# Memory attention and SwiGLU on one core: keys and values of the last four batches handled inside the first sweep, and one sweep for each of the last two pairs

## The chip, the cores and the metric

The kernel runs on one core of one Trainium2 chip. The metric is the device time of one execution in microseconds (us). The kernel before takes 942.52 us, the median of three runs that lie between 942.49 and 943.4. About 0.2% is what a measurement of this kernel can tell from no change.

A core has engines with queues of their own: TensorE (PE, matmuls and transposes; PEld are its weight loads), VectorE (DVE), ScalarE (ACT), GpSimd (POOL) and SyncE (SP), which here issues all transfers. Each queue is worked off in the order in which it was written. Matmuls write to PSUM, which PE, DVE and ACT reach; all else is in SBUF.

## The reference, cut to what matters

Eight batches, 8 heads, 576 rows, head size 64, 32 memory slots; then a SwiGLU layer with 512 inputs and 1536 hidden units on all 4608 rows:

```python
a = softmax(phi, axis=2)                       # over the 576 rows
k_m, v_m = a^T k, a^T v                        # 32 x 64 for each batch and head
attn = softmax(q k_m^T / 8, axis=-1)           # 576 x 32
x = attn v_m                                   # heads side by side: 4608 x 512
xn = x / sqrt(mean(x*x) + 1e-6) * rms_g
out = (silu(xn @ w_gate) * (xn @ w_val)) @ w_out
```

The three weights come as 64-bit floats. TensorE works in a 32-bit form in which a number is carried as a high and a low part, so each large product is three matmuls (high-high, high-low, low-high).

## The kernel before, in words

The batches are worked in four **pairs** (two batches each). `v_m` is never multiplied out over the rows: for each pair and each block of 128 hidden units the kernel first multiplies `v_m` with the weights (tile `vp`, lines 837 to 869), and then the attention weights of the pair (`at_hi`, `at_lo`) with that product (tiles `pg` and `pv`, lines 871 to 915).

**Part 1** (lines 428 to 821) does, for all eight batches, the keys and values: load `phi`, `k`, `v`; take the maximum of `phi` over rows (`prep`: DVE reduce `mc`, PE transpose `mt`, DVE `mx` and `mb`, PE transpose `mr`, DVE subtract, ACT exp into `e_bd`, POOL partial sums `es`); 72 matmuls into `kvp` and 24 for the sums (`kv_steps`); DVE `si`, `im`, `kb`, `vb`; PE transposes `kvt`; copies to `km` and `vt`. For batches 4 to 7, `km` stays in SBUF (`km_late`), and the rest goes to DRAM. For pairs 0 and 1 it also does queries, scores, softmax and `x_steps`, which ends in a short chain of small DVE instructions for `rinv` (lines 257 to 278), three transposes `rp`, and the split into `at_hi` and `at_lo`.

**The sweeps** (lines 824 to 1088) are 48 steps of 128 hidden units for one pair: pairs 0 and 1 in turn through all 12 blocks (steps 0 to 23, the first sweep), then pairs 2 and 3 in turn (steps 24 to 47). In each step PE does 12 matmuls for `vp`, 48 for `pg` and `pv`, and every two steps 54 for the output (`po`). `vp` has one buffer; ACT copies it to `xf` in three instructions and casts it to `xh`, POOL subtracts for `xl` (`evac`, lines 858 to 868). DVE multiplies `pv` with the activated `pg` into `hf` and adds `po` to `acc`; `pg`, `pv` and `po` have two buffers each.

Inside the first sweep run two more things. **Weight conversion** (`convert`, lines 335 to 414): 36 pieces of 512 columns are turned from 64-bit floats into the two parts; a piece is seven instructions on DVE. Converted weights are also written to DRAM and read back (`reload`) in the second sweep. **Attention of pairs 2 and 3** (`attend_steps`, `x2`).

Every step has a place on a time axis (tables in `PRM`), and the steps are issued in that order; a scheduler then puts the instructions of an engine into a fixed order of its own, by its own model of when each can run. The tables were written for that.

Of the kernel before, what the change touches and what calls it, by code (L numbers as in the profile page):

```python
# [19 lines left out]
WB = 3  # L20
PRM = dict(
    K_AT=[12.08, 15.05, 41.68, 67.52, 100.72, 122.69, 147.6, 167.28],
    KP=0.82,
    POST=[-0.15, 3.05, 3.9, 7.72, 15.27, 21.96],
    P1=4.13,
    PREP=[-1.56, 0.79, 2.32, 3.9, 18.7],
    PD=[2.1, 11.67, 7.79, 18.42, 7.54, 2.17],
    EXP=[1.89, 13.89, 3.07, 6.96, 11.93, 1.72],
    ES=1.16,
    PH=[9.86, 15.89, 41.23, 73.43, 103.91, 132.92],  # L30
    S_AT=[32.67, 47.44, 51.02, 69.42, 103.56, 112.2, 119.41, 123.39],
    KD=[-29.43, -117.84, -35.71, -6.98, -5.97, -14.4, 0.19, -2.47, -27.9, -16.32, -19.75, -7.2, -11.66, -11.87, -26.49, -25.1, -22.49, -18.77, -23.35, -24.43, -11.42, -13.48, -5.56, -9.46, -16.01, -22.32, -10.3, -18.0, -66.41, -9.39, -2.35, -17.36],
    QD=[5.05, 0.01, 25.98, 0.89, 23.44, 5.14, 27.93, 20.58],
    PD0=0.96,
# [3 lines left out]
    SO=[3.76, 13.53, 20.6, 28.62],  # L38
    X_AT=[102.5, 152.9],
    XP=1.78,  # L40
    LAG=0.79,
    CV=114.79,
    CP=3.53,
    CV2=155.67,
    CP2=0.05,
# [3 lines left out]
    ESN=[3, 3, 2, 3, 3, 3, 2, 3],  # L49
    QX=[2, 8],  # L50
# [13 lines left out]
    SU=[1.874, 3.014, 5.716, 6.6, 9.746, 12.208, 13.357, 15.533],  # L64
    AO=[0.162, 0.169, 0.192, 0.276, 0.385, 0.474, 0.562, 0.581, 0.59, 0.601, 0.728, 0.804, 1.158, 1.217],
    XB=[17.199, 22.916],
    XS=[0.1086, 0.0359],
    XM=[21.887, 24.858],
    XN=[0.012, 0.176, 0.184, 0.33, 0.33, 0.566, 0.596, 0.699, 0.766],
    LV=[22.571, 24.198],  # L70
# [21 lines left out]
def kernel(  # L92
# [44 lines left out]
    gram = {}  # L137
    gb = persist.tile([P, 2, 2, P], F32, name="gb")
# [171 lines left out]
    def first_weights():  # L310
        return (
            [lambda: (load_w(0, 0), load_w(1, 0))]
            + convert(0, 0) + [lambda: load_w(0, 1)] + convert(1, 0) + [lambda: load_w(1, 1)]
        )
# [101 lines left out]
    def reload(kind, n):  # L416

        if kind == 2:
            t = [wp[1].tile([P, 512], F32R, tag=x, name=f"{x}{n}", bufs=2) for x in ("oh", "ol")]
# [8 lines left out]
    with ExitStack() as c1:  # L428
# [6 lines left out]
        ones = sb.tile([P, 1], F32, name="ones", bufs=1)  # L435
        nc.vector.memset(ones, 1.0)
        hmask = sb.tile([P, 2], F32, name="hmask", bufs=1)
# [10 lines left out]

        rg = [sb.tile([P, HP], F32, name=f"rg{i}", bufs=1) for i in range(2)]
# [51 lines left out]
        def prep(b, hp0=0, hp1=HP):  # L501
# [55 lines left out]
            def s4():  # L557
                e = e_bd[b % 2]
                n = PRM["ESN"][b]
# [12 lines left out]
        def kv_steps(b):  # L572
# [59 lines left out]
            def post2():  # L632
                tp = st.pop(("kvt", b))
                km = km_late.get(b)
                if km is None:
                    km = sb.tile([P, HP, 64], F32, tag="km", name=f"km{b}", bufs=4)
# [482 lines left out]
```

## Time and profile before

| stage (us from the start) | PE busy | DVE busy | granted PE clock |
|---|---|---|---|
| part 1, 0 to 158 | 118.2 | 114.3 | 0.87 |
| 158 to 200 | 31.3 | 38.1 | 0.84 |
| 200 to 450 | 224.4 | 205.7 | 0.98 |
| 450 to 569 | 113.5 | 61.8 | 0.97 |
| second sweep, 569 to 940.2 | 364.6 | 140.4 | 1.00 |

The profiled execution took 941.95 us in all, and its span from first to last instruction is 940.2 us; 1.75 us lie around it. The first `pg` matmul of step 0 starts at 158.2 us, and that of step 24 at 569.2 us; these two moments bound the first sweep. A row of the profile names line, engine, operation and tile; "busy, mean ns | idle before <- who ended it" follows. PE busy is no measure of useful work, since matmuls overlap.

### The profile page before, as it was taken

The page shows a single profiled execution, that of the slowest core. Times are in us where ns is not written, and L with a number is a line of the kernel's source. Part 1 is how long each engine was busy: PE and PEld are TensorE (multiplying, and loading weights), DVE is VectorE, ACT ScalarE, POOL GpSimd, SP SyncE. Part 2 cuts the span into 40 slices and gives each one's busy share as a digit, 9 for nine tenths or more (in the row PEclk, how much of TensorE's full clock was granted, in tenths as well). Part 3 has the DMA queues.
Part 4 walks back from the last instruction along what each step waited for, and adds up shares of the span by engine and source line. Part 5 has one row for each costly group of instructions (what it writes and reads, how often), then busy time and mean ns, then how long its engine had stood idle before and what let it go on. Part 6 is the DMA issues. An engine that isn't in the chain of part 4 may idle for free.

```text
span 940.2 us, 15899 instructions
## 1 busy us (share of the span) xinstructions
PE 852.0 (91%) x6207; PEld 756.7 (80%) x6207; DVE 560.4 (60%) x998; ACT 433.2 (46%) x743; POOL 408.7 (43%) x290
## 2 busy tenths in 40 slices
PE   5799676689889899897799999999999999999998
PEld 4678565679779688786699898798989999999996
DVE  5487969895897976969843463643333333333333
ACT  2566333656547546465454354343343443443430
POOL 2365636562653554454344354253333423433421
PEclk9889877899899999999899999999999999999999
DMA  8997644452343623434223215341202212030046
GB/s 282 254 288 237 225 134 131 143 159 66 98 158 83 187 76 83 161 100 152 90 64 102 68 60 134 85 115 45 90 1 69 67 36 100 1 129 7 1 107 140
DMA packets 85667, 106.42 MB, mean 113 GB/s; under 512 B 38996, under 2 KB 56920, under 8 KB 85592
## 3 DMA queue, kind: packets, MB, share of 16 engines
q1 hardware_dynamic: 85592, 105.41, 37.7%
q8 instruction: 49, 0.80, 0.4%
q14 instruction: 26, 0.21, 0.1%
HBM read 73.93 MB, written 31.46 MB: 112 GB/s over the span
## 4 chain that ended last, share of the span: by engine, by line
PE 69%; DVE 20%; DMA 3%; issue 3%; ACT 3%; POOL 1%; SPq 0%; DVEq 0%; ACTq 0%; POOLq 0%
PE po L931 28%; PE pv L889 13%; PE pg L889 13%; PE vp L852 5%; DVE mi L369 3%; DVE mi L365 3%; DVE w L385 2%; PE kvp L583 2%; PE xp L235 2%; DVE ex L345 2%; DMA phi<-in_phi_dram 2%; DVE ex L358 1%; DVE acc L938 1%; DVE ex L357 1%; DVE ex L352 1%
## 5 line engine op out<-in xcount | busy, mean ns | idle before, releaser
L912 POOL TENSOR_TENSOR hl<-hf,hh 128x512 fp32r<-128x512 f32 (+1 forms) x96 | 143.6, 1496 | 235.1 <-ACT hh L911 180.6
L938 DVE TENSOR_TENSOR acc<-po,acc 128x512 f32<-128x512 f32 x180 | 123.8, 689 | 165.4 <-PE po L931 165.2
L931 PE MATMUL po<-oh,hh 128*128 128x512 f32 x432 | 174.4, 405 | 14.3 <-DVE acc L938 12.0
L867 POOL TENSOR_TENSOR xl<-xf,xh 128x1024 fp32r<-128x1024 f32 x48 | 118.3, 2465 | 137.4 <-ACT xh L866 73.6
L931 PE MATMUL po<-oh,hl 128*128 128x512 f32 x432 | 172.0, 398 | 0.0
L931 PE MATMUL po<-ol,hh 128*128 128x512 f32 x432 | 171.5, 397 | 0.0
L897 ACT ACTIVATE sg<-pg 128x256 f32<-128x256 f32 x192 | 78.5, 411 | 189.3 <-PE pg L889 175.5
L898 DVE TENSOR_TENSOR hf<-pv,sg 128x256 f32<-128x256 f32 x192 | 85.4, 452 | 106.9 <-PE pv L889 65.2
L931 PEld LDWEIGHTS po<-oh,hh 128*128 128x128 f32 x432 | 81.7, 190 | 30.5 <-DVE acc L938 15.3
L889 PE MATMUL pv<-ath,xh 128*128 128x320 f32 (+1 forms) x384 | 87.2, 306 | 15.6 <-DVE hf L898 15.6
L852 PE MATMUL vp<-wh,vm 128*128 128x256 f32 x384 | 89.0, 297 | 11.1 <-ACT xf L863 10.8
L931 PEld LDWEIGHTS po<-oh,hl 128*128 128x128 f32 x432 | 81.9, 190 | 19.5
L911 ACT CAST hh<-hf 128x512 fp32r<-128x512 f32 (+1 forms) x96 | 64.6, 674 | 70.7 <-DVE hf L898 40.0
L931 PEld LDWEIGHTS po<-ol,hh 128*128 128x128 f32 x432 | 82.0, 190 | 10.9
L889 PE MATMUL pg<-ath,xh 128*128 128x320 f32 (+1 forms) x384 | 87.2, 302 | 1.1 <-ACT sg L897 1.1
L889 PE MATMUL pg<-ath,xl 128*128 128x320 f32 (+1 forms) x384 | 85.7, 298 | 0.0
L889 PE MATMUL pg<-atl,xh 128*128 128x320 f32 (+1 forms) x384 | 85.7, 299 | 0.0
L889 PE MATMUL pv<-atl,xh 128*128 128x320 f32 (+1 forms) x384 | 83.8, 298 | 0.0
L889 PE MATMUL pv<-ath,xl 128*128 128x320 f32 (+1 forms) x384 | 83.7, 296 | 0.0
L889 PEld LDWEIGHTS pv<-ath,xh 128*128 128x128 f32 x384 | 63.6, 193 | 23.0 <-DVE hf L898 18.4
L852 PEld LDWEIGHTS vp<-wh,vm 128*128 128x128 f32 x384 | 68.8, 201 | 14.1 <-ACT xf L863 11.7
L889 PEld LDWEIGHTS pg<-ath,xh 128*128 128x128 f32 x384 | 64.9, 192 | 7.3 <-ACT sg L897 1.5
(133 smaller groups left out, 1522.7 us busy)
## 6 DMA issues: line engine op xcount, KB each, us to landing
kv<-in_k_dram SPq DMA_DIRECT2D x32, 288.0 KB, 6.2
kv<-in_v_dram SPq DMA_DIRECT2D x32, 288.0 KB, 6.2
out_dram<-acc SPq DMA_DIRECT2D x72, 128.0 KB, 2.4
raw<-in_moe_w_gate_dram SPq DMA_DIRECT2D x12, 512.0 KB, 4.1
raw<-in_moe_w_val_dram SPq DMA_DIRECT2D x12, 512.0 KB, 4.1
wd<-wh SPq DMA_DIRECT2D x12, 512.0 KB, 3.5
wd<-wl SPq DMA_DIRECT2D x12, 512.0 KB, 3.3
raw<-in_moe_w_out_dram SPq DMA_DIRECT2D x12, 512.0 KB, 3.6
```

Of the source, the lines that this page charges most:

```text
L235: nc.tensor.matmul(xp[64 * j:64 * j + 64, P * cc:P * cc + P], st["at"][:, t, cc, 64 * j:64 * j + 64], gb[:, j, cc], start=True, stop=True,)
L365: V.tensor_scalar(out=m, in0=d["raw"][:, :, 1], scalar1=0xFFFFF, scalar2=None, op0=ALU.bitwise_and)
L369: V.scalar_tensor_tensor(out=mf, in0=d["raw"].bitcast(U32)[:, :, 0], scalar=2.0 ** -32, in1=m, op0=ALU.mult, op1=ALU.add,)
L852: nc.tensor.matmul(vp[:, cc, e, :], lhs(l), r[:, 2 * cc + e, :], start=(n == 0), stop=(n == 2),)
L867: nc.gpsimd.tensor_tensor(out=xl, in0=xf, in1=xh.bitcast(F32), op=ALU.subtract)
L889: nc.tensor.matmul(pt[:, :N], l[:, cc, b, half * P:half * P + P], r[:, b, cc, t0:t0 + n, :].rearrange("p t x -> p (t x)"), start=(m == 0), ...
L897: nc.scalar.activation(sg[:, :N], pg[:, :N], AF.Silu)
L898: nc.vector.tensor_tensor(out=hf[:, :, b, :], in0=pv[:, :N].rearrange("p (t x) -> p t x", x=64), in1=sg[:, :N].rearrange("p (t x) -> p t x ...
L911: nc.scalar.copy(hh, hv)
L912: nc.gpsimd.tensor_tensor(out=hl, in0=hv, in1=hh.bitcast(F32), op=ALU.subtract)
L931: nc.tensor.matmul(po, l[:, tt, :], r, start=(m == 0), stop=(m == 5))
L938: nc.vector.tensor_tensor(out=accs[key], in0=po, in1=accs[key], op=ALU.add)
```

## The change

- Part 1 handles batches 0 to 3 only. Loads come in a fixed list, 1.1 units apart.
- Keys and values of batches 4 to 7 are done by the new `late_kv` in the first sweep, at steps 0.3, 2.1, 9.5 and 11.3. It shares PSUM buffers with `po`, and holds two of a batch's four (k, v) tiles at a time, in the buffers `qr` and `qT`, so the second half is fetched when the first has been used.
- Pairs 2 and 3 have a sweep each (steps 24 to 35 and 36 to 47). Converted weights are now read back for each of the 24 steps instead of for 12 blocks.
- `evac`: `xf` is gone. For each half of the partitions ACT casts `vp` to `xh`, and DVE, no longer POOL, subtracts for `xl`, straight from PSUM.
- The tables of times are new, buffers for converted weights `w` go from three to two, and some choices of part 1 that were set batch by batch are uniform.

```diff
-WB = 3
+WB = 2
-    K_AT=[12.08, 15.05, 41.68, 67.52, 100.72, 122.69, 147.6, 167.28],
+    K_AT=[12.0, 22.0, 36.0, 46.0],
-    X_AT=[102.5, 152.9],
-    XP=1.78,
+    X_AT=[47.5, 73.5],
+    XP=0.87,
+    KV=[0.3, 2.1, 9.5, 11.3],
...
-    NS = (NP // G) * NU * G * 2
+    NS = NP * NJ
+    UNITS = [(p, u) for u in range(NU) for p in range(G)] + [(p, u) for p in range(G, NP) for u in range(NU)]
...
         def evac():
             vp = vw[i][0]
-            xf = sb.tile([P, 2, 2, 256], F32, tag="xf", name=f"xf{i}")
-            nc.scalar.copy(xf[0:64], vp[0:64])
-            for b in range(2):
-                nc.scalar.copy(xf[64:128, :, b, :], vp[64:128, :, 1 - b, :])
...
-            nc.scalar.copy(xh, xf)
-            nc.gpsimd.tensor_tensor(out=xl, in0=xf, in1=xh.bitcast(F32), op=ALU.subtract)
+            for h in range(2):
+                rows = slice(64 * h, 64 * h + 64)
+                src = vp[rows, :, ::-1, :] if h else vp[rows]
+                nc.scalar.copy(xh[rows], src)
+                nc.vector.tensor_tensor(out=xl[rows], in0=src, in1=xh[rows].bitcast(F32), op=ALU.subtract)
...
+    def late_kv(b):
...
+        def fetch_kv(cc):
+            def f():
+                for par in range(2):
+                    hp = 2 * cc + (par ^ j)
+                    d[par] = t = sb.tile([P, 2, S], F32, tag=("qr", "qT")[par], name=f"kv{b}_{hp}")
+                    for i, src in enumerate((k, v)):
+                        nc.sync.dma_start(
...
+        def mm(cc):
+            def f():
+                d["kvp"] = kvp = o_tile(f"kvp{b}_{cc}")
+                for c in range(NT):
+                    for par in range(2):
+                        nc.tensor.matmul(
+                            kvp[64 * par:64 * par + 64, 0:128], late["e"][:, 2 * cc + (par ^ j), c, :],
+                            d[par][:, :, 64 * c:64 * c + 64], start=(c == 0), stop=(c == NT - 1),
+                        )
+            return f
...
+        return [
+            lambda: (fetch_phi(), fetch_kv(0)()), top, turn_mc, top2, turn_mb, less, exp, some,
+            mm(0), sums(0), norm(0), fetch_kv(1), mm(1), sums(1), norm(1), turn, post, self_products, post2,
+        ]
...
-    NALL = (NP // G) * NJ
...
+        n = where(i)[3]
+        if n >= NJ:
+            ev.append((i - PRM["WR"], lambda n=n: reload(0, n)))
+            ev.append((i - i % 2 - PRM["OR"] + 0.01 * (i % 2), lambda n=n: reload(2, n)))
...
+    for a, p in enumerate(PRM["KV"]):
+        ev += place(p, PRM["KO"], late_kv(2 * G + a))
```

How the change moves instructions is seen best at two places. The first is VectorE's queue at the end of part 1, in the middle of the chain for `rinv` of pair 1 (lines 274 to 276 in both kernels), on which `rp`, the split of pair 1 and, by PE's order, the first `vp` wait. Before:

```order
L274 TENSOR_TENSOR u_1666<-rinv_71 128x9
L275 TENSOR_TENSOR u_1666<-u_1666,m_1660 128x9
L276 SCALAR_TENSOR_TENSOR rinv_71<-u_1666,rinv_71 128x9
L274 TENSOR_TENSOR u_1666<-rinv_71 128x9
L606 TENSOR_SCALAR si_1746<-kvp_1621 128x2
L275 TENSOR_TENSOR u_1666<-u_1666,m_1660 128x9
L607 RECIPROCAL si_1746<-si_1746 128x2
L276 SCALAR_TENSOR_TENSOR rinv_71<-u_1666,rinv_71 128x9
```

After (`raw`, `ex`, `mi`, `w` are tiles of weight conversion; the number behind the name is the block):

```order
L275 TENSOR_TENSOR u_1302<-u_1302,m_1296 128x9
L384 TENSOR_TENSOR w_1_1571<-mi_1_1565,ex_1_1554 128x512
L276 SCALAR_TENSOR_TENSOR rinv_75<-u_1302,rinv_75 128x9
L344 TENSOR_SCALAR ex_2_1718<-raw_1398 128x512
L364 TENSOR_SCALAR mi_2_1728<-raw_1398 128x512
L274 TENSOR_TENSOR u_1302<-rinv_75 128x9
L351 TENSOR_SCALAR ex_2_1718<-ex_2_1718 128x512
L368 SCALAR_TENSOR_TENSOR mi_2_1728<-raw_1398,mi_2_1728 128x512
L275 TENSOR_TENSOR u_1302<-u_1302,m_1296 128x9
L356 TENSOR_SCALAR ex_2_1718<-ex_2_1718 128x512
L276 SCALAR_TENSOR_TENSOR rinv_75<-u_1302,rinv_75 128x9
```

Between the links of the chain now stand instructions of four weight pieces; ahead of the first `hf` of the sweep nine pieces are begun, where seven were begun before.

The second place is TensorE's queue in step 1, the second half of its `pg` and `pv` (L889 before, L875 after). Before:

```order
L889 MATMUL pv_01_1995<-ath_1393,xl_1900 128x256 x2
L889 MATMUL pg_10_2016<-ath_1393,xh_1899 128x320 x2
L889 MATMUL pg_10_2016<-atl_1394,xh_1899 128x320 x2
L889 MATMUL pg_10_2016<-ath_1393,xl_1900 128x320 x2
L889 MATMUL pv_10_2017<-ath_1393,xh_1899 128x320 x2
```

After (`kvp` is the product of `e_late` with the keys and values `kv` of batch 4; `ones` stands for the sums):

```order
L875 MATMUL pv_01_1578<-ath_1158,xl_1466 128x256 x2
L1019 MATMUL kvp_0_1598<-kv_1_1456,e_late 64x128
L1031 MATMUL kvp_0_1598<-ones,es_1573 64x1 x2
L1031 MATMUL kvp_0_1598<-ones,e_late 64x1
L1031 MATMUL kvp_0_1598<-ones,es_1573 64x1 x2
L1031 MATMUL kvp_0_1598<-ones,e_late 64x1
L1019 MATMUL kvp_1_1656<-kv_2_1632,e_late 64x128
L875 MATMUL pg_10_1639<-ath_1158,xh_1465 128x320 x2
```

The matmuls of batch 4 now stand between those of the sweep, and the first one of the second half (`kvp_1`, which reads the newly fetched `kv_2`) stands directly behind the last ones of the first half, ahead of the rest of step 1.

259 lines of the change are left out of this document (175 added, 84 removed).

## The prediction

> **What bounds the kernel now.** I read the slices of the page first, then busy time by stage, then what ended TensorE's idle time, then single stretches. The slices are 23.5 us each:
>
> ```profile
> PE   5799676689889899897799999999999999999998
> DVE  5487969895897976969843463643333333333333
> DMA  8997644452343623434223215341202212030046
> ```
>
> For the first two slices the transfers are full and DVE is half idle; from the third on DVE is the fuller one, and DMA falls. The stages in numbers:
>
> ```profile
> core 0: us, PE busy (x) PEld busy (x) DVE busy (x) ACT busy (x) POOL busy (x), PEclk, DMA share, GB/s
> 0.00:158.00 158.00, 118.19 (x1497) 101.44 (x1497) 114.31 (x240) 71.73 (x130) 80.20 (x87) 0.87 0.74 221
> 158.00:200.00 42.00, 31.27 (x184) 29.14 (x182) 38.12 (x46) 22.96 (x39) 24.77 (x14) 0.84 0.47 155
> 200.00:450.00 250.00, 224.42 (x1540) 198.86 (x1541) 205.73 (x330) 141.26 (x232) 118.27 (x71) 0.98 0.40 118
> 450.00:569.00 119.00, 113.52 (x748) 100.19 (x747) 61.77 (x125) 54.77 (x99) 53.32 (x41) 0.97 0.27 87
> 569.00:940.20 371.20, 364.58 (x2244) 327.08 (x2242) 140.43 (x261) 142.46 (x245) 132.10 (x79) 1.00 0.24 68
> ```
>
> The second sweep is PE end to end (6.6 us idle of 371), so nothing is to be won there, and its work doesn't change. The first sweep runs from here to here:
>
> ```profile
> 158.19 0.79 PE L889 MATMUL pg<-ath,xh 128*128 128x256 f32 x2
> 569.21 0.40 PE L889 MATMUL pg<-ath,xh 128*128 128x256 f32 x2
> ```
>
> In its 411 us PE is busy 369.2 and idle 41.8, and the idle time has these owners (groups of PE in that stretch):
>
> ```profile
> L931 PE MATMUL po<-oh,hh 128*128 128x512 f32 x186 | 76.8, 413 | 13.2 <-DVE acc L938 10.9 <-DVE ex L1006 1.4 <-DVE acc L936 0.4
> L852 PE MATMUL vp<-wh,vm 128*128 128x256 f32 x201 | 46.3, 299 | 6.1 <-ACT xf L863 6.1
> L889 PE MATMUL pv<-ath,xh 128*128 128x256 f32 (+1 forms) x192 | 45.9, 316 | 15.2 <-DVE hf L898 15.2
> L995 PE MATMUL S<-km,qT 128*64 128x64 f32 x288 | 11.7, 227 | 5.7 <-DVE acc L938 2.6 <-DVE acc L936 2.5 <-ACT qT L983 0.6
> ```
>
> So the first sweep is PE-bound, with DVE late by a tenth. Why late, one case shows:
>
> ```profile
> 239.17 2.82 POOL L867 TENSOR_TENSOR xl<-xf,xh 128x1024 fp32r<-128x1024 f32 x1
> 239.79 2.48 DVE L345 TENSOR_SCALAR ex<-raw 128x512 int32<-128x512 int32 x1
> 244.13 0.80 PE L889 MATMUL pv<-ath,xh 128*128 128x256 f32 x2 [3.27 <-DVE hf L898]
> ...
> L345 DVE TENSOR_SCALAR ex<-raw x36: 359/428/2648, 88.2 to 460.2; 128x512 int32<-128x512 int32 x36
> L938 DVE TENSOR_TENSOR acc<-po,acc x180: 628/692/693, 285.3 to 935.5; 128x512 f32<-128x512 f32 x180
> ```
>
> A conversion instruction of 0.43 us takes 2.48 beside POOL's `xl` of 2.82 us, and `hf` behind it is late; `acc`, which reads PSUM, never lasts over 0.69.
>
> **Term 1, part 1 and the start of the sweep: -12 us.** Removed from DVE are four batches, each by these rows an eighth of 38.6 us (the first two are over nine instructions), so 4.8:
>
> ```profile
> L509 DVE TENSOR_REDUCE mc<-phi 128x128 f32<-128x1152 f32 (+1 forms) x9 | 17.4, 1937 | 6.8 <-DMA phi<-in_phi_dram 6.8
> L542 DVE TENSOR_TENSOR phi<-phi,mr 128x1152 f32<-128x1152 f32 (+1 forms) x9 | 11.0, 1217 | 12.1 <-PE mr L533 12.1
> L609 DVE TENSOR_TENSOR im<-si,hmask 128x4 f32<-128x4 f32 x8 | 3.5, 441 | 0.1
> L615 DVE TENSOR_TENSOR kb<-kvp,im 128x256 f32<-128x256 f32 x8 | 3.4, 423 | 0.3
> L615 DVE TENSOR_TENSOR vb<-kvp,im 128x256 f32<-128x256 f32 x8 | 3.3, 414 | 0.0
> ```
>
> That is -19.3. But the order puts work in its place, ahead of the first `hf`: two more weight pieces, batch 4's `mc` and `phi` (3.2), and two of the new subtractions. A piece, from the first to the last of its seven instructions:
>
> ```profile
> 156.57 0.57 DVE L345 TENSOR_SCALAR ex<-raw 128x512 int32<-128x512 int32 x1
> 162.83 0.69 DVE L385 TENSOR_TENSOR w<-mi,ex 128x512 f32<-128x512 f32 x1
> 163.56 0.43 DVE L345 TENSOR_SCALAR ex<-raw 128x512 int32<-128x512 int32 x1
> 167.49 0.69 DVE L385 TENSOR_TENSOR w<-mi,ex 128x512 f32<-128x512 f32 x1
> ```
>
> So 7.0 us beside POOL, 4.6 with less of it: 11 for two. A subtraction of 64x1024 is nearest to this one, which also reads PSUM and 1024 columns:
>
> ```profile
> L212 DVE TENSOR_TENSOR at<-at,rp 128x1024 f32<-128x1024 f32 x8 | 9.6, 1213 | 1.8 <-PE rp L204 1.8
> ```
>
> 2.4 for two. Net for DVE -19.3 + 11 + 3.2 + 2.4 = -2.7, say -3. Its idle time, 43.7 us of the 158, lies mostly in the first two slices, where loads of batches 0 and 1 are awaited, and these remain. Against that, two waits at the start go, of PE for `vp`'s one buffer, which is held by `xf`, behind POOL's `xl`:
>
> ```profile
> 155.34 0.58 PE L852 MATMUL vp<-wh,vm 128*128 128x256 f32 x1 [4.70 <-ACT xf L863]
> 169.21 0.58 PE L852 MATMUL vp<-wh,vm 128*128 128x256 f32 x1 [6.13 <-ACT xf L863]
> ```
>
> I credit 9 of their 10.8 us; the rest stays as a wait for ACT's two casts and DVE. Bounds: +5, if the conversion between the links of the `rinv` chain costs more than the four batches; -45, if part 1 hung on its transfers. Four batches are 11.8 MB (k and v 288 KB each and four times, phi 576 KB), 53 us at 221 GB/s. I take the value near DVE's end, as DVE is the full one when part 1 ends.
>
> **Term 2, PE's work for batches 4 to 7: +25 us.** In part 1 it lay in PE's idle time; in the first sweep PE is the bound.
>
> ```profile
> 138.50 2.46 PE L583 MATMUL kvp<-kv,e_bd 128*64 128x128 f32 x41
> ...
> L583 PE MATMUL kvp<-kv,e_bd 128*64 128x128 f32 x576 | 47.8, 316 | 0.5 <-ACT e_bd L552 0.5
> L598 PE MATMUL kvp<-ones,e_bd 128*64 128x1 f32 x96 | 9.6, 208 | 0.0
> L598 PE MATMUL kvp<-ones,es 128*64 128x1 f32 x128 | 9.5, 204 | 0.0
> ```
>
> Lower end: 60 ns each in the dense stretch, 288 of them, 17 us. Upper: half of the three groups, 33. Dense matmuls plus sums and some ten transposes a batch lie between: 25.
>
> **Term 3, new waits in PE's queue: +5 us.** The second half of a batch's keys and values is fetched only when the first half's matmuls have left the buffers, and its first matmul stands close behind; `mr` stands close behind `mt`, with two DVE instructions between. What is queued behind is the whole sweep. A load of this kind lands after
>
> ```profile
> kv<-in_k_dram SPq DMA_DIRECT2D x32, 288.0 KB, 6.2
> ```
>
> 6.2 us in the full queue of part 1. About 40 sweep matmuls stand between release and use at one place, and fewer at others. Bounds: 0, all covered; +25, 6.2 us a batch uncovered. I take the low side, since the sweep moves 118 GB/s, not 221.
>
> The row for the clock after the 3.27 us wait above is
>
> ```profile
> 243.00:250.00 7.00, 5.87 (x22) 5.58 (x23) 6.36 (x12) 5.77 (x9) 2.24 (x2) 0.51 0.20 77
> ```
>
> half the clock for 7 us, so 3.4 us lost beside the wait. The Trainium skill ("TensorE: Matmul & The Clock Gate", What's actually happening) has it that an idle window of about 3.4 us drops the array to half rate until it has again been busy as long; this trace agrees. By that rule one long wait a batch would add 4 x 3.4 = 14 us, and the sum would be 972.
>
> **Term 4, DVE in the first sweep: -2 us.** Added: the subtraction, 24 steps x 2.4 = 58 us; four batches, 19 less the 3 above; removed: two pieces, 11. Also removed, from POOL:
>
> ```profile
> L867 POOL TENSOR_TENSOR xl<-xf,xh 128x1024 fp32r<-128x1024 f32 x25 | 63.0, 2520 | 62.8 <-ACT xh L866 32.9 <-PE pg L889 8.6 <-DVE ex L358 7.4
> ```
>
> its longest instruction, and with it part of what holds the conversion up (2.4 us a piece between the two pieces above, 65 us over 27 pieces; I take 25). DVE goes from 305.6 us of 411 (74%) to 306 + 58 + 16 - 11 - 25 = 344 of some 430 (80%). Shorter holds make PE's 41.8 us less, at best by 20; more load makes them more, by some 25 at worst. I set -2. The read-back of weights for pair 3, 18 MB more over 370 us, lies beside a stage in which DMA is 0.24 busy: 0. Two buffers for `w`, not three: 0, as POOL, which frees them, is emptier.
>
> **Sum.** -12 + 25 + 5 - 2 = +16. The profiled execution took 941.95, 0.6 below the median; 941.95 + 16 = 957.95, so **958 us**: slower.
>
> **The rivals.**
>
> *A, faster: part 1 hung on its transfers.* Mechanism: with 11.8 MB gone everything after the first 47 us starts earlier, and the weight pieces that the order moves forward fall into gaps of DVE. For it: the first slices. Against: DVE 0.6 to 0.9 in the slices that follow, and conversion inside the `rinv` chain. Term 1 then is -40: 930. It wins from the point where `pg` starts before about 130 us.
>
> *B, about even or faster: the holds by POOL were most of PE's waits.* Term 4 is then -20, and the sum -2: 940. For it: the case at 240 us. Against: DVE's new 58 us stand in the same queue as `hf` and `acc`. The Trainium skill ("SBUF — State Buffer", Who interferes with whom) says that a DVE instruction in a two-port mode, or with two SBUF inputs, and one of POOL shut each other out for a whole instruction, and that one SBUF input alone doesn't; by that rule the new subtraction, which reads PSUM and SBUF, neither waits for POOL nor holds it up. The trace agrees for `acc`.
>
> *C, slower still: DVE becomes the bound of the first sweep.* If nothing of the holds goes, DVE has 306 + 58 + 16 - 11 = 369 us; at 200 to 450, with 0.82 busy, PE lost a tenth, so at that share the sweep lasts 450, not 411: +39, with term 1 -12 and 5 for the fetches: 974; with term 1 at 0, 986.
>
> That the change doesn't do what it says is excluded by the order.
>
> **How the numbers follow.** Forecast (its own range 946 to 970): 0.50. A: 0.20. B: 0.15. C: 0.15. The range must reach into A and C: 924 to 986. Faster by over 0.2% (under 940.6; that is about what a measurement of this kernel can tell from no change): A, and two thirds of B, 0.30. Within 0.2%: 0.08, from B and the low edge of the forecast. Slower: 0.62.
>
> **What would show it.** Term 1: the first `pg` at 140 to 152 us; at 130 or less A holds. Term 2: PE busy in the first sweep 25 us longer. Term 3: PE waits ended by `kv` loads or `mb`, some 5 us together. Term 4: PE idle in the first sweep near 42 us, DVE near 80% busy. From the first `pg` of step 24 to the end, 371 us as before; if that stage grows, the read-back of weights is not hidden and the forecast is wrong at a place where I set nothing.

## The result, and the profile after

The changed kernel takes 976.14 us, the median of four runs between 974.53 and 977.55. The kernel before took 942.5 beside it. The ratio is 1.0354, with a 95% interval of 1.0336 to 1.0372: slower by 33.6 us. The prediction had 958, 15.5 above the kernel before, so the sign was right and the size was under half.

The stages of the kernel after (time by stage, columns as in the prediction):

```profile
core 0: us, PE busy (x) PEld busy (x) DVE busy (x) ACT busy (x) POOL busy (x), PEclk, DMA share, GB/s
0.00:156.70 156.70, 96.47 (x1015) 78.59 (x1015) 99.51 (x233) 63.56 (x115) 65.69 (x75) 0.73 0.58 175
...
604.60:975.80 371.20, 365.90 (x2254) 329.26 (x2254) 193.14 (x308) 122.54 (x205) 83.21 (x62) 1.00 0.37 113
...
156.70:604.60 447.90, 404.35 (x2907) 354.16 (x2907) 335.89 (x575) 209.19 (x336) 141.72 (x110) 0.95 0.40 125
```

The first `pg` starts at 156.7 us, against 158.2 before: 1.5 earlier, where the prediction set 12. The first sweep lasts 447.9 us, against 411.0: 36.9 longer, where the prediction set 28. From step 24 on it is 371.2 against 371.0: the weights read back for the two separate sweeps (113 GB/s in place of 68) are hidden, as predicted. In the profiled executions these are -1.5 + 36.9 + 0.2 = 35.6 us, the difference of the spans 975.8 and 940.2.

In the first sweep PE is busy 404.35 us (369.2 before) and idle 43.5 (41.8). The idle time has other owners than before. Groups of PE in that stretch, kernel after:

```profile
L917 PE MATMUL po<-oh,hh 128*128 128x512 f32 x186 | 79.9, 430 | 12.2 <-DVE acc L924 8.4 <-DVE ex L1144 1.8 <-ACT at L194 0.7
L875 PE MATMUL pv<-ath,xh 128*128 128x256 f32 (+1 forms) x192 | 44.0, 311 | 1.3 <-DVE hf L884 1.3
...
L1019 PE MATMUL kvp<-kv,e_late 128*64 128x128 f32 x288 | 19.7, 277 | 7.9 <-DMA kv<-in_v_dram 5.5 <-DVE acc L924 1.7 <-DVE acc L922 0.7
...
L1031 PE MATMUL kvp<-ones,es 128*64 128x1 f32 x64 | 4.4, 197 | 0.0
L1031 PE MATMUL kvp<-ones,e_late 128*64 128x1 f32 x32 | 3.5, 197 | 0.0
...
L1060 PE MATMUL kvt<-ident,lakb 128*128 128x128 f32 x8 | 2.1, 305 | 4.2 <-DVE lakb L1048 4.2
L1080 PE MATMUL self<-vt 128*64 128x64 f32 x32 | 1.8, 234 | 0.0
L1060 PE MATMUL kvt<-ident,lbkb 128*128 128x128 f32 x8 | 1.8, 310 | 0.0
...
L993 PE MATMUL mr<-ident,mb 128*128 128x128 f32 x3 | 1.0, 338 | 1.6 <-DVE mb L989 1.6
L981 PE MATMUL mt<-ident,mc 128*128 128x128 f32 x3 | 1.0, 337 | 4.3 <-DVE mc L975 4.3
```

The wait for `hf` has gone from 15.2 us to 1.3. In its place stand 18.0 us at the late keys and values (7.9 + 4.2 + 1.6 + 4.3), and the busy times of these rows add up to 35.3 us (19.7 + 4.4 + 3.5 + 2.1 + 1.8 + 1.8 + 1.0 + 1.0). That sum is too high, for rows of overlapping matmuls count the same time more than once. All instructions of the tile `kvp` together, products and sums, are busy 23.20 us and not 27.6 (the same stretch, that tile alone):

```profile
156.70:604.60 447.90, 23.20 (x384) 20.39 (x384) 5.21 (x24) 0.95 0.40 125
```

By tile, `kvt` is busy 3.19 us, `self` 1.81, `mt` and `mr` 1.01 each. So the work of the four batches is at most 30.2 us on PE.

Part 1 shows why its end hardly moved. In the kernel before, the chain for `rinv` of pair 1 ran on VectorE almost without a stranger in it (timeline of DVE, before):

```profile
139.29 0.17 DVE L259 TENSOR_SCALAR m<-ssq 128x9 f32<-128x9 f32 x1
...
143.43 0.17 DVE L276 SCALAR_TENSOR_TENSOR rinv<-u,rinv 128x9 f32<-128x9 f32 x1
```

After, it begins 9.8 us earlier and ends 1.4 us later (the same timeline, after, with PE's wait for it):

```profile
129.48 0.17 DVE L259 TENSOR_SCALAR m<-ssq 128x9 f32<-128x9 f32 x1
...
131.03 1.49 DVE L351 TENSOR_SCALAR ex<-ex 128x512 int32<-128x512 int32 x1
...
133.53 0.16 DVE L274 TENSOR_TENSOR u<-rinv 128x9 f32<-128x9 f32 x1
133.60 2.08 DVE L975 TENSOR_REDUCE mc<-phi 128x128 f32<-128x1152 f32 x1
135.60 0.68 DVE L357 SCALAR_TENSOR_TENSOR ex<-raw,ex 128x512 int32<-128x512 int32 x1
136.20 0.16 DVE L275 TENSOR_TENSOR u<-u,m 128x9 f32<-128x9 f32 x1
...
144.78 0.16 DVE L276 SCALAR_TENSOR_TENSOR rinv<-u,rinv 128x9 f32<-128x9 f32 x1
...
145.00 1.97 PE L204 MATMUL rp<-ident,rinv 128*128 128x128 f32 x8 [16.09 <-DVE rinv L276]
```

The chain takes 15.5 us in place of 4.3, with weight pieces and batch 4's `mc` between its links, and TensorE waits 16.1 us for it.

### The profile page after: what moved, and what is told of

Read it like the earlier page. It is cut to its first block, busy times and chain, and to the rows that moved or that the text cites. A ratio compares the mean times of both kernels' runs of the same rounds, so it can differ in the third digit from the quotient of the medians.

```text
span 975.8 us, 15862 instructions
## 1 busy us (share of the span) xinstructions
PE 866.7 (89%) x6175; PEld 762.0 (78%) x6175; DVE 628.5 (64%) x1114; ACT 395.3 (41%) x655; POOL 290.6 (30%) x245
## 4 chain that ended last, share of the span: by engine, by line
PE 65%; DVE 15%; issue 3%; ACT 2%; DMA 1%; POOL 0%; DVEq 0%; ACTq 0%; POOLq 0%
PE po L917 27%; PE pg L875 14%; PE pv L875 14%; PE vp L839 6%; DVE mi L364 2%; DVE ex L344 2%; DVE mi L368 2%; DVE xl L853 2%; DVE acc L924 1%; PE kvp L1019 1%; PE xp L235 1%; DVE ex L351 1%; DVE hf L884 1%; DVE ex L357 1%; ACT L1151 1%
## 5 line engine op out<-in xcount | busy, mean ns | idle before, releaser
L898 POOL TENSOR_TENSOR hl<-hf,hh 128x512 fp32r<-128x512 f32 (+1 forms) x96 | 140.7, 1466 | 460.3 <-ACT hh L897 457.4
L917 PE MATMUL po<-oh,hh 128*128 128x512 f32 x324 | 134.7, 416 | 12.2 <-DVE acc L924 8.4
L853 DVE TENSOR_TENSOR xl<-vp,xh 64x1024 fp32r<-64x1024 f32 x96 | 117.1, 1220 | 34.5 <-ACT xh L852 33.1
L852 ACT CAST xh<-vp 64x1024 fp32r<-64x1024 f32 x96 | 96.8, 1008 | 86.3 <-PE vp L839 55.0
L917 PE MATMUL po<-ol,hh 128*128 128x512 f32 x324 | 130.9, 404 | 0.0
L917 PE MATMUL po<-oh,hl 128*128 128x512 f32 x324 | 130.7, 404 | 0.0
L875 PE MATMUL pg<-ath,xh 128*128 128x320 f32 (+1 forms) x384 | 87.8, 307 | 2.8 <-ACT xh L852 2.2
L839 PE MATMUL vp<-wh,vm 128*128 128x256 f32 x384 | 85.2, 291 | 5.0 <-ACT wh L401 2.7
L875 PE MATMUL pv<-ath,xh 128*128 128x320 f32 (+1 forms) x384 | 85.9, 303 | 1.3 <-DVE hf L884 1.3
L875 PE MATMUL pg<-atl,xh 128*128 128x320 f32 (+1 forms) x384 | 86.5, 300 | 0.0
L875 PE MATMUL pg<-ath,xl 128*128 128x320 f32 (+1 forms) x384 | 85.8, 297 | 0.6 <-DVE xl L853 0.6
L875 PE MATMUL pv<-atl,xh 128*128 128x320 f32 (+1 forms) x384 | 84.8, 300 | 0.0
L917 PEld LDWEIGHTS po<-oh,hh 128*128 128x128 f32 x324 | 62.7, 194 | 27.1 <-DVE acc L924 11.6
L875 PE MATMUL pv<-ath,xl 128*128 128x320 f32 (+1 forms) x384 | 83.8, 297 | 0.0
L917 PEld LDWEIGHTS po<-oh,hl 128*128 128x128 f32 x324 | 62.8, 194 | 14.9
L875 PEld LDWEIGHTS pg<-ath,xh 128*128 128x128 f32 x384 | 65.7, 195 | 9.8 <-ACT xh L852 3.3
L917 PEld LDWEIGHTS po<-ol,hh 128*128 128x128 f32 x324 | 62.9, 194 | 9.0
```

The costliest lines, as they stand in the source:

```text
L839: nc.tensor.matmul(vp[:, cc, e, :], lhs(l), r[:, 2 * cc + e, :], start=(m == 0), stop=(m == 2),)
L852: nc.scalar.copy(xh[rows], src)
L853: nc.vector.tensor_tensor(out=xl[rows], in0=src, in1=xh[rows].bitcast(F32), op=ALU.subtract)
L875: nc.tensor.matmul(pt[:, :N], l[:, cc, b, half * P:half * P + P], r[:, b, cc, t0:t0 + n, :].rearrange("p t x -> p (t x)"), start=(m == 0), ...
L898: nc.gpsimd.tensor_tensor(out=hl, in0=hv, in1=hh.bitcast(F32), op=ALU.subtract)
L917: nc.tensor.matmul(po, l[:, tt, :], r, start=(m == 0), stop=(m == 5))
```

## The experiments

Two bases are used: the kernel before (labels with b) and the kernel after (labels with a). "Without the four batches" means that the keys, values and gram products of batches 4 to 7 are left out and those of batches 0 to 3 are used in their place. The edits are shown cut, with ... for what is left out. All times are compared with the kernel before in the same comparison; "us" is the ratio less one, times 942.5.

| run | median | ratio, 95% interval | us | first `pg` | to step 24 |
|---|---|---|---|---|---|
| the change (after) | 976.14 | 1.0354 [1.0336, 1.0372] | +33.4 | 156.7 | 447.9 |
| b_evac | 920.38 | 0.9788 [0.9772, 0.9805] | -20.0 | 155.3 | 383.9 |
| b_evac2 | 921.10 | 0.9777 [0.9761, 0.9792] | -21.0 | 155.1 | 386.7 |
| b_evac_start | 920.28 | 0.9770 [0.9746, 0.9795] | -21.7 | 148.2 | 391.8 |
| b_nokv | 931.16 | 0.9896 [0.9875, 0.9917] | -9.8 | 155.5 | 402.6 |
| b_evac_nokv | 920.04 | 0.9767 [0.9744, 0.9789] | -22.0 | 154.0 | 384.2 |
| b_evac_nokv_chain | 907.51 | 0.9631 [0.9611, 0.9652] | -34.8 | 145.6 | 380.7 |
| a_nokv | 926.94 | 0.9851 [0.9832, 0.9869] | -14.0 | 155.3 | 399.7 |
| a_nokv_tab | 925.89 | 0.9827 [0.9811, 0.9843] | -16.3 | 156.8 | 393.2 |
| a_nokv_wb3 | 920.12 | 0.9768 [0.9738, 0.9799] | -21.9 | 158.3 | 389.8 |
| a_nokv_chain | 920.50 | 0.9781 [0.9753, 0.9808] | -20.6 | 148.6 | 398.9 |
| a_chain | 968.52 | 1.0289 [1.0270, 1.0308] | +27.2 | 152.3 | 443.9 |
| a_mr | 974.93 | 1.0341 [1.0318, 1.0365] | +32.1 | 150.6 | 451.0 |
| a_start | 974.81 | 1.0337 [1.0318, 1.0356] | +31.8 | 141.4 | 459.3 |
| a_ko | 971.36 | 1.0312 [1.0291, 1.0333] | +29.4 | 155.5 | 444.7 |
| a_ko_chain | 969.74 | 1.0307 [1.0276, 1.0338] | +28.9 | 153.7 | 445.8 |

"To step 24" is the time between the first `pg` of step 0 and that of step 24. In the five runs with b_evac in their name, and in a_nokv_tab, the scheduler puts some matmuls of the first sweep behind that `pg`: from there to the end they take 376 to 380 us, where all others take 371 to 372, so their first sweep is 5 to 9 us longer than the table says. The medians are not touched by that.

### The new evac alone (b_evac)

```diff
-            nc.scalar.copy(xf[0:64], vp[0:64])
-            for b in range(2):
-                nc.scalar.copy(xf[64:128, :, b, :], vp[64:128, :, 1 - b, :])
...
-            nc.scalar.copy(xh, xf)
-            nc.gpsimd.tensor_tensor(out=xl, in0=xf, in1=xh.bitcast(F32), op=ALU.subtract)
+            for h in range(2):
+                rows = slice(64 * h, 64 * h + 64)
+                src = vp[rows, :, ::-1, :] if h else vp[rows]
+                nc.scalar.copy(xh[rows], src)
+                nc.vector.tensor_tensor(out=xl[rows], in0=src, in1=xh[rows].bitcast(F32), op=ALU.subtract)
```

> The kernel before with only the new evac (ACT casts vp to xh in two halves, DVE subtracts from PSUM, no xf, nothing on POOL); tables and everything else as before. Theory E (in the kernel after, this part helps and something else costs): the waits of PE for hf (15.2 us before, 1.3 after) and for xf at vp (10.8 with those ahead of the sweep) go, so 942.5 - 15 to 20 = 922 to 928, with the second sweep, 6.6 us idle, unchanged at 371. Rival D (the subtraction on DVE is what makes the kernel after slower): 48 x 1.22 = 58 us more of DVE in each of the two sweeps stands in the queue of hf and acc; waits of PE for acc and hf grow by 15 us or more in the first sweep, 955 or over.

It is 20.0 us faster than the kernel before and beats both kernels. Time by stage, first sweep of b_evac:

```profile
155.30:539.20 383.90, 359.08 (x2445) 320.24 (x2446) 324.55 (x548) 190.90 (x318) 128.37 (x96) 0.98 0.36 116
```

PE is idle 24.8 us there (383.90 - 359.08), although DVE now is busy 85% of it. PE's waits in that stretch (us in all, times, longest):

```profile
PE pg L888 <- ACT xh L865: 7.5, 1, 7.5
PE qtp L976 <- DVE acc L935: 6.0, 3, 2.2
PE pg L888 <- ACT sg L896: 5.0, 3, 2.9
...
PE pv L888 <- DVE hf L897: 0.8, 2, 0.5
```

The wait for `hf` is down to 0.8 us. So theory E holds and rival D falls: in the kernel before, the subtraction on DVE costs nothing that shows. The edit also takes the copies to `xf` off ACT, and PE's wait of 6.1 us for `xf` in the first sweep goes with them; how much of the 20 us is POOL's holds and how much is these copies was not told apart. The change contains an edit worth 20 us, and the rest of it costs 53.

### Both casts first (b_evac2)

```diff
...
-                nc.scalar.copy(xh[rows], src)
-                nc.vector.tensor_tensor(out=xl[rows], in0=src, in1=xh[rows].bitcast(F32), op=ALU.subtract)
+                nc.scalar.copy(xh[64 * h:64 * h + 64], src[h])
+            for h in range(2):
+                rows = slice(64 * h, 64 * h + 64)
+                nc.vector.tensor_tensor(out=xl[rows], in0=src[h], in1=xh[rows].bitcast(F32), op=ALU.subtract)
```

> The kernel before with the new evac, but both casts of ACT written ahead of both subtractions of DVE. In b_evac the second cast waited for the first subtraction 15 times in the first sweep, 15.6 us together, and pg waited 7.5 us for xh. Theory E2 (that order is part of the price of evac): xh is ready a subtraction earlier, those waits go and the total is 912 to 917. Rival (vp and xh were early enough nearly everywhere, 7.5 us of it are one case): 918 to 922.

-21.0 us against -20.0: no difference that can be told. The rival holds; the waits for `xh` are made up for elsewhere.

### The four batches left out of the kernel after (a_nokv)

```diff
...
-    for a, p in enumerate(PRM["KV"]):
-        ev += place(p, PRM["KO"], late_kv(2 * G + a))
```

> The kernel after without late_kv: batches 4 to 7 use the keys, values and gram products that part 1 makes of batches 0 to 3 (four more small ACT copies and eight transfers in part 1), so that the work on keys and values of batches 4 to 7 is left out altogether. Theory K (the late keys and values are the loss): PE loses 25 to 35 us of work in the first sweep and some 18 us of waits that stand at kvp, kvt, mt, mr; some of these waits only replaced others, so the first sweep falls from 448 to 405 to 415, and the total to 935 to 945. Rival D (DVE with subtraction and conversion sets the first sweep): only DVE's 16 us of these batches go, the first sweep is 430 or longer, the total 955 or over. The first pg stays at 155 to 157 by both.

The total falls by 47 us (+33.4 to -14.0). First sweep, a_nokv:

```profile
155.30:555.00 399.70, 368.65 (x2468) 325.32 (x2468) 317.54 (x522) 187.24 (x310) 124.49 (x92) 0.97 0.35 110
```

Against the kernel after, PE has 35.7 us less to do (404.35 - 368.65) and 12.5 less idle time (43.55 - 31.05): 48.2 us for four batches, 12 each. Theory K holds with a larger price than it named. Of the 35.7 at most 30.2 are the late batches' own instructions. The other 5.5 us or more lie in the sweep's own matmuls, of which there are as many as in a_nokv and which take longer: all of `po` is busy 154.31 us, against 150.84 there. Half clock fits that: by the granted clocks, 0.05 of 447.9 us are lost in the one and 0.03 of 399.7 in the other, so some 10 us of clock time more (the clock is given to 0.01, so give or take 4), of which a part falls on idle time.

### The four batches left out of part 1 of the kernel before (b_nokv, b_evac_nokv)

```diff
...
-        for b in range(B):
+        for b in range(2 * G):
             steps, post = kv_steps(b)
...
```

> The kernel before, with batches 4 to 7 left out of part 1: they use what part 1 makes of batches 0 to 3 (four small ACT copies and eight transfers more), so that their keys and values are left out altogether; tables, evac and sweeps as before. It measures what part 1 gives up when four batches leave it, which the prediction put at 12 us with the new order. Theory S (DVE's queue fills with weight pieces as soon as room is there; they stand between the links of the rinv chain here too): the first pg at 145 to 158, and the total 925 to 942, since two or more pieces less are left for the sweep. Rival A (part 1 hung on its transfers): the first pg at 130 or earlier, the total 915 or less.

> The kernel before with the new evac and with batches 4 to 7 left out of part 1 (as in b_nokv). If evac (-20 us) and the four batches less in part 1 (-9.6 us) add up: 911 us, and the 16 us by which a_nokv (926.9) stands above it are the price of the rest of the change (its tables of times, two buffers for w, the sweeps). If they don't add up, since both take load from the same waits of the first sweep: 917 to 922, and the rest costs under 10.

With the old evac, leaving them out brings 9.8 us; with the new one, where only their removal differs from b_evac, 2.0 us, within the intervals of no difference. The two edits don't add up. The first `pg` comes at 155.5 and 154.0, so rival A is out: part 1 doesn't hang on the transfers of these batches. What b_nokv gains lies mostly in its first sweep (402.6 in place of 411.0); what it is there wasn't settled. Why so little comes of it at the start, DVE's timeline of b_evac_nokv shows:

```profile
127.76 0.68 DVE L369 SCALAR_TENSOR_TENSOR mi<-raw,mi 128x512 f32<-128x512 uint32 x1
128.36 0.16 DVE L268 TENSOR_SCALAR rinv<-rinv 128x9 int32<-128x9 int32 x1
...
135.16 0.16 DVE L275 TENSOR_TENSOR u<-u,m 128x9 f32<-128x9 f32 x1
136.10 0.43 DVE L345 TENSOR_SCALAR ex<-raw 128x512 int32<-128x512 int32 x1 [0.77 <-DMA raw<-in_moe_w_val_dram]
136.44 0.42 DVE L365 TENSOR_SCALAR mi<-raw 128x512 int32<-128x512 int32 x1
136.78 0.16 DVE L276 SCALAR_TENSOR_TENSOR rinv<-u,rinv 128x9 f32<-128x9 f32 x1
```

The scheduler's order puts weight pieces between the links here too, though the tables are those of the kernel before; once DVE even waits in the chain for a weight to land (0.77 us).

### The chain kept clear, without the four batches (b_evac_nokv_chain)

```diff
...
+        if 0 < a < 8:
+            c[:5] = [behind(f) for f in c[:5]]
```

`behind` queues what it wraps behind the last `rinv` instruction of pair 1 on DVE; it sets the order and adds no wait.

> The kernel before with the new evac, batches 4 to 7 left out of part 1 (b_evac_nokv, 920.0), and in addition seven weight pieces queued behind the last link of the rinv chain of pair 1; in b_evac_nokv they stood between its links, and DVE waited 6.3 us there for a transfer of raw. Theory S (leaving four batches out of part 1 is worth Term 1's 10 us only if the chain of pair 1 stays clear): the first pg at 141 to 146, total 908 to 913. Rival L (part 1's end is no bound of the total, since the pieces are owed to the sweep): the first pg as early, total 916 to 921.

In the expectation, 6.3 us is the time that a transfer of `raw` takes in the chain of waits; DVE's own wait there was the 0.77 quoted above. The run is 12.8 us faster than b_evac_nokv. The chain takes 4.8 us (timeline of DVE):

```profile
124.63 0.17 DVE L259 TENSOR_SCALAR m<-ssq 128x9 f32<-128x9 f32 x1
...
129.29 0.17 DVE L276 SCALAR_TENSOR_TENSOR rinv<-u,rinv 128x9 f32<-128x9 f32 x1
```

The first `pg` comes at 145.6, and what is gained there is kept to the end of the first sweep and beyond (time by stage):

```profile
145.60:526.30 380.70, 356.80 (x2442) 318.36 (x2443) 314.93 (x531) 188.90 (x314) 126.94 (x95) 0.98 0.35 110
```

Against b_evac, which has all eight batches in part 1 and a chain as clear (4.3 us), it is 14.8 us faster. So leaving four batches out of part 1 is worth 12 us or more, as Term 1 had it, but only when nothing is put between the links of the last chain.

### The chain kept clear in the kernel after (a_chain, a_mr, a_start)

a_chain is the edit above, with batch 4's `mc` behind the chain as well. a_mr puts `mc` behind the second subtraction of step 0, and `mt` and `mr` behind the first `pg` and `pv`. a_start puts the pieces behind that subtraction too, and both casts first. The line for batch 4 is the same in a_mr and a_start:

```diff
...
-            lambda: (fetch_phi(), fetch_kv(0)()), top, turn_mc, top2, turn_mb, less, exp, some,
+            lambda: (fetch_phi(), fetch_kv(0)()), behind(top, first_xl), behind(turn_mc, first), top2, behind(turn_mb, first), less, exp, some,
```

> The kernel after, with the DVE instructions of seven weight pieces and of batch 4's mc queued behind the last link of the chain for rinv of pair 1 instead of between its links; nothing else is changed. Theory S (the pieces between the links hold up the start): the chain takes 4 us instead of 15, the first pg comes at 144 to 147 instead of 156.7, and the total falls by 8 to 11 us, to 965 to 968. Rival L (the pieces are only paid later, since the same DVE work is still ahead of the blocks 2 and 3): the first pg comes as early, but step 5 to 8 of the sweep waits for its weights and the total falls by under 4 us, to 972 to 976. Rival O (something else, a transfer or the ACT and POOL work on the split of pair 1, holds the first pg): it stays at 153 or later.

> As the run that kept the pieces out of the rinv chain (a_chain: first pg 152.3 us, where mr of batch 4 stands ahead of it in the queue of PE and waits 6.9 us for mb), and in addition batch 4's mc is queued behind the second subtraction of step 0 on DVE, and its mt and mr behind the first pg and pv of step 0 on PE. Theory S (the start was held by work that the new order put ahead of it, first in DVE's queue, then in that of PE): the first pg at 144 to 148, which is Term 1's 12 us, and the total 958 to 964. Rival L (only moved on: mr's wait now stands in step 1, and the sweep loses it there): the first pg as early, the total 966 to 970.

> The kernel after with the start cleared all the way: the DVE instructions of seven weight pieces and batch 4's mc behind the second subtraction of step 0 (in a_mr a whole piece stood ahead of the first subtraction, and pg waited 8.0 us for xh), both casts of xh ahead of both subtractions, batch 4's mt and mr behind the first pg and pv of step 0. Theory S: the first pg at 141 to 147, and the total 10 us or more below the kernel after, 960 to 966. Rival L (given back: in a_mr the first pg came 6 us earlier, the first sweep lasted 3 us longer, and the median fell by 1): the first pg as early, but steps 2 to 8 wait for the weights whose pieces now come later, total 970 to 976.

a_chain takes 6.2 us off the kernel after. Its first `pg` comes 4.4 us earlier, not 10, for the next wait stands ready in PE's queue (timeline of PE, a_chain):

```profile
150.17 0.47 PE L1003 MATMUL mr<-ident,mb 128*128 128x128 f32 x1 [6.87 <-DVE mb L999]
152.34 0.80 PE L885 MATMUL pg<-ath,xh 128*128 128x256 f32 x2 [1.70 <-ACT xh L862]
```

a_mr misses both its expectations, with the first `pg` at 150.6 and 974.9 us. With `mr` out of the way the next wait appears, `xh` behind a subtraction that stands behind a weight piece (timeline of DVE, then PE's waits, a_mr):

```profile
140.20 1.40 DVE L354 TENSOR_SCALAR ex<-raw 128x512 int32<-128x512 int32 x1
...
148.28 1.21 DVE L863 TENSOR_TENSOR xl<-vp,xh 64x1024 fp32r<-64x1024 f32 x1
```

```profile
PE pg L887 <- ACT xh L862: 8.0, 1, 8.0
```

And with that one gone too, `pg` starts at 141.4, 15 us earlier than after, and little of it is left at the end: a_mr and a_start end within 2 us of the kernel after. The first loss lies where the pieces, which were owed, are made up for. In the first 72 us of a_start's sweep DVE is the full engine:

```profile
141.40:213.40 72.00, 63.30 (x454) 58.94 (x455) 66.91 (x107) 38.21 (x61) 26.59 (x18) 0.90 0.40 134
```

DVE is busy 66.9 of 72.0 us there, and the lead falls from 15.3 us at step 0 to 5.2 at step 5 and 2.9 at step 6. But it doesn't stay there: it is 10.3 us at step 12 and 9.2 at step 20, and falls to 3.9 at step 24. Between steps 6 and 12 a_start has no wait for `kv`, where the kernel after has one of 5.5 us; from step 20 to 24 PE is idle 6.8 us, against 3.0. So the debt on DVE fits the first loss, and why the lead comes back and goes again was not settled. Theory S holds for the start and not for the total. Rival L holds in that the gain is given back, for a_start in its time too; but it had the sweep wait for converted weights, and PE waits for none of them in the first 98 us of a_start's sweep.

### The same on the other kernels (a_nokv_chain, b_evac_start)

The edit of a_chain in a_nokv, and the first eight pieces behind step 0's second subtraction in b_evac2.

> The kernel after without the keys and values of batches 4 to 7 (a_nokv, 926.9), with seven weight pieces queued behind the last link of the rinv chain of pair 1. In the kernel before without these batches this one edit took 12.5 us off (b_evac_nokv_chain, 907.5), in the kernel after with them 7.6 (a_chain). Theory S (what clears the start is kept where nothing of batches 4 to 7 stands in the sweep): 914 to 918. Rival (the kernel after gives it back for another reason, its part 1 or its tables): 920 to 927.

> The kernel before with the new evac, both casts ahead of both subtractions (b_evac2, 921.1), and the first eight weight pieces of the sweep queued behind the second subtraction of step 0 on DVE; one stood between the split of pair 1 and that subtraction, part of another ahead of it. Theory S: the first pg at 148 to 152 instead of 155, total 914 to 918, the fastest of all. Rival L (given back when the pieces come later): 919 to 923.

a_nokv_chain gains 6.6 us on a_nokv, less than the 9 to 13 of theory S, and its 920.5 us lie at the low end of the rival's range. b_evac_start starts 7 us earlier and ends as b_evac2 does: rival L again.

### More room for the late chain (a_ko, a_ko_chain)

```diff
-    KV=[0.3, 2.1, 9.5, 11.3],
-    KO=[0.0, 0.3, 0.45, 0.5, 0.6, 0.65, 0.8, 0.95, 1.05, 1.1, 1.2, 1.25, 1.4, 1.45, 1.55, 1.6, 1.75, 1.9, 2.0],
-    SU=[4.0, 5.3, 6.7, 8.1, 13.2, 14.6, 16.0, 17.4],
+    KV=[0.3, 2.8, 9.5, 12.0],
+    KO=[0.0, 0.3, 0.5, 0.6, 0.85, 0.95, 1.1, 1.2, 1.25, 1.3, 1.35, 1.4, 1.8, 1.85, 1.9, 2.1, 2.2, 2.3, 2.4],
+    SU=[5.3, 6.3, 7.2, 8.1, 14.5, 15.4, 16.4, 17.4],
```

> The kernel after with other times for late_kv: more room between mc, mt, mb and mr, and between the fetch of the second half and its matmuls (64 others between kvp_0 and kvp_1 of batch 6 where there were 11; 42 to 90 for the others), and the queries of pairs 2 and 3 placed later to make room. Same work. Theory K (the waits that stand at the late chain, some 18 us of 43.5 us idle in the first sweep, are the new loss beside PE's work): PE idle 30 to 35, total 964 to 969. Rival M (the waits only move, since DVE is late by its whole load): the waits at kvp, mt, mr go and others at po, qtp and pg grow, PE idle 40 or more, total 972 to 979.

> The kernel after with both repairs that brought something: the spaced times of late_kv (a_ko, 971.4, 4.8 less) and the pieces behind the rinv chain (a_chain, 968.5, 7.6 less). If the two are independent: 962 to 966. If both pay into the same lateness of DVE: 967 to 971. In both cases above the kernel before, since the work of the four batches on PE in the sweep, some 35 us, stays.

a_ko is 4.0 us better than the kernel after. Its first sweep, and then PE's longest waits in it:

```profile
155.50:600.10 444.60, 400.17 (x2906) 348.05 (x2906) 338.27 (x575) 209.04 (x336) 142.07 (x109) 0.97 0.40 126
```

```profile
PE pg L875 <- ACT xh L852: 8.1, 7, 2.2
PE mt L981 <- DVE mc L975: 5.1, 1, 5.1
```

The 5.5 us wait for `kv` is gone, and PE is idle 44.4 us as before (43.5): the waits moved, to `xh` above all, as rival M had it, while the total came out between the two expectations. What is gained is clock (0.97 in place of 0.95, with PE's busy time 4.2 us less). With both repairs together the kernel isn't better than with a_chain alone, so the two pay into the same lateness, as the second expectation had it. All repairs stay 27 us or more above the kernel before, since the late batches' work on PE stays.

### The rest of the change (a_nokv_tab, a_nokv_wb3)

```diff
-WB = 2
+WB = 3
```

> The kernel after without the keys and values of batches 4 to 7 (a_nokv, 926.9), with the times of the kernel before for the attention of pairs 2 and 3 (SU, XB, XS, XM, LV), which start at step 1.9 instead of 4.0. Theory: the 7 us between a_nokv and b_evac_nokv (920.0) come from attention being pushed later and closer together: 919 to 923. Rival: they come from the other tables of part 1 or from two buffers for w: 925 to 929.

> The kernel after without the keys and values of batches 4 to 7 (a_nokv, 926.9), with three buffers for converted weights w as in the kernel before. It stands 6.9 us above b_evac_nokv (920.0), and the times for attention were not the cause (a_nokv_tab, 925.9). Theory W (the third buffer, which the prediction set at 0): 919 to 923. Rival (the tables and the load list of part 1): 925 to 929.

The earlier times for the attention of pairs 2 and 3 gain 2.3 us, within the intervals. The third buffer for converted weights gains 7.9 us on a_nokv, with intervals of 2 and 3 us, and closes the gap to b_evac_nokv. PE's longest waits in the first sweep, first of a_nokv, then of a_nokv_wb3:

```profile
PE po L921 <- DVE acc L928: 11.8, 11, 2.8
PE qtp L1119 <- DVE acc L928: 6.3, 3, 4.5
```

```profile
PE qtp L1119 <- DVE acc L928: 2.3, 2, 1.8
...
PE po L921 <- DVE acc L928: 1.8, 2, 1.2
```

The scheduler makes another order of DVE's queue with the third buffer, and 14 us of these two waits go. Others come in their place (the longest is 6.5 us, of `pg` for `xh`): PE's idle time in the first sweep falls by 3.0 us only (31.05 to 28.1), and its busy time by 6.9 (368.65 to 361.7), at a clock of 0.98 in place of 0.97. How much of the gain is the buffer and how much the order was not told apart.

## Why the prediction had the sign right and the size wrong

Set side by side, all from the profiled executions, with a_nokv as the border between the terms:

| step | predicted | measured | from |
|---|---|---|---|
| Term 1, start | -12 | -1.5 | first `pg` 156.7 against 158.2 |
| Term 2, work on PE | +25 | +35.7 | PE busy, after less a_nokv |
| Term 3, waits in PE's queue | +5 | +12.5 | PE idle, after less a_nokv |
| Term 4, DVE | -2 | -11.3 | first sweep, a_nokv less before |
| second stage | 0 | +0.2 | 371.2 against 371.0 |
| sum | +16 | +35.6 | |

The borders are a convention. The late batches' work on DVE (335.9 us less the 317.5 of a_nokv) is in the rows of Terms 2 and 3, though the prediction had it in Term 4.

**Term 1 failed in its logic.** It took part 1's end to follow the sum of DVE's work and two waits for `xf`: less work, fewer waits, an earlier end. Both waits are gone, and DVE's busy time before the first `pg` fell by 15.0 us (114.5 to 99.5). The second wait, 6.13 us at 169, stood behind the first `pg`, so the table counts it in the first sweep; the first `hf`, up to which the term was reckoned, does come 9.0 us earlier (162.5 against 171.5). But the end of part 1 hangs on a chain of small dependent instructions. Four batches fewer let that chain begin 10 us earlier (129.5 against 139.3), and then pieces stood between its links. The order quoted ahead of the prediction shows them, and I set them only as the bound (+5) at which the gain is lost. b_evac_nokv and b_evac_nokv_chain show it by itself: 2 us without, 12.8 more with a clear chain. In the kernel after, clearing it brought 6.2.

**Term 2 was mis-sized, and it left out the clock.** I took 25 between 17 and 33. The late batches' own instructions are busy for at most 30.2 us: the products and sums 23.2, and the transposes and small products 7.0, of which the upper end of the bounds held none. The rest of the 35.7, 5.5 us or more, is no work of theirs. The sweep's own matmuls take longer, which fits the slower clock, and that was priced in the prediction and left out of its sum.

**Term 3 was mis-sized.** The fetch was awaited once, 5.5 us, near the row of 6.2 that the prediction took from part 1; `kvt` and `mt` waited 4 us each, and I had named `mr` and the fetch alone. Of the 18 us at these places 12.5 are net. Its companion, the clock, I left out of the sum. The 5.55 us wait for `kv` (timeline of PE), and then the clock behind it (time by stage), kernel after:

```profile
372.24 0.66 PE L1019 MATMUL kvp<-kv,e_late 128*64 128x128 f32 x2 [5.55 <-DMA kv<-in_v_dram]
```

```profile
367.00:374.00 7.00, 1.56 (x6) 1.19 (x7) 6.88 (x13) 3.70 (x5) 1.52 (x1) 0.71 0.77 249
```

0.71 of the clock in these 7 us, and over the sweep about 10 us of clock time (give or take 4) were lost that a_nokv doesn't lose. What of them falls on working matmuls is inside Term 2's 35.7, not beside it, since slow matmuls count as busy; what falls on idle time costs nothing. By the Trainium skill ("TensorE: Matmul & The Clock Gate", What's actually happening) an idle window of about 3.4 us brings the half clock; the 14 us, an estimate worked out in the prediction from that window for four long waits, stands beside these 10. In one point the trace decides otherwise than the prediction, which said that it agrees: shorter waits brought the half clock too. The row that the prediction shows follows a wait of 3.27 us, and in the kernel after a wait of 3.01 us, from 476.2 on, has a clock of 0.50 behind it, from 479.1 on. And as PE was busy 5.87 of the 7 us of the prediction's row, the loss beside the wait was some 3 us, not 3.4.

**Term 4 had the right parts and the wrong weight.** The subtraction takes 1.22 us, as estimated; DVE was busy 335.9 us of the sweep, where I had 344. Its share is 75%, not 80, since the sweep is longer. But the load cost less than the new `evac` gained: its edit is worth 20 us by itself (b_evac), as much as rival B set, to which I gave 0.15. PE's wait for `hf` fell from 15.2 us to 0.8 by it, which is B's mechanism, though the copies to `xf` left with it. I set this gain against DVE's added 58 us and let them cancel, and no run shows such a cost. And two buffers for `w`, which I set at 0 because POOL is emptier, cost some 8 us, with the order that comes with them (a_nokv_wb3). In totals the steps are -20.0 for `evac`, -2.0 for the four batches out of part 1 (b_evac_nokv) and +7.9 for two buffers, which leaves 0.1 for the rest of the way to a_nokv's -14.0. The late batches then add 47.4. These prices hold in this order, since the edits don't add up.

Rival A is out: without the four batches' loads `pg` starts at 154 us, and at 145.6 with the chain clear, where A had 130 or less. Rival C named the right time, 974 to 986, for a wrong reason: DVE didn't become the bound of the sweep, it was 75% busy. That hit was luck.

## What to carry to other kernels

Work that lies in an engine's idle time costs little, and the same work in a stretch where that engine is the bound costs all of its instructions, small transposes and sums included, and some waits and clock on top: here 12 us a batch, against 12 to 15 for all four. Before you credit a stage with the work taken out of it, find the chain that ends it, and look at what the new order puts between its links. A change of several edits should be tried edit by edit: one of these is worth 20 us alone and was buried under 53.

## What the runs showed of the hardware

A DVE subtraction that reads PSUM and one SBUF input was never held up beside POOL, and the instruction `ex<-raw` of the conversion is held up less once POOL's 2.5 us subtraction is gone (instructions of one tile and of one line, kernel after; ns min/median/max, first and last start; between them one subtraction and POOL's beside it, from the timelines):

```profile
L853 DVE TENSOR_TENSOR xl<-vp,xh x96: 1154/1223/1231, 154.4 to 936.9; 64x1024 fp32r<-64x1024 f32 x96
...
554.45 1.21 DVE L853 TENSOR_TENSOR xl<-vp,xh 64x1024 fp32r<-64x1024 f32 x1
554.22 1.55 POOL L898 TENSOR_TENSOR hl<-hf,hh 128x640 fp32r<-128x640 f32 x1 [1.03 <-ACT hh L897]
...
L344 DVE TENSOR_SCALAR ex<-raw x36: 405/428/1499, 33.5 to 550.0; 128x512 int32<-128x512 int32 x36
```

None of 96 took over 1.23 us, while the longest `ex<-raw` fell from 2.65 us to 1.50; its mean was 0.85 us before and 0.59 in b_evac, where only `evac` differs. The first agrees with the Trainium skill ("SBUF — State Buffer", Who interferes with whom), by which a DVE instruction with at most one SBUF input, outside the two-port modes, doesn't contend with POOL. I had not expected how much the new `evac` is worth: with the subtraction moved to the fuller engine, PE's idle time in the first sweep fell from 41.8 us to 24.8 (b_evac).
